# Four shared products of a Strassen-Winograd stage through one PSUM bank pair, sums moved from GpSimd to VectorE, and the first output steps prepared in another order

## The chip, the core and the metric

One core of a Trainium2 chip. The metric is the device time of one execution in microseconds, lower is better. Durations in the rows come from one profiled execution, counted from the start of its span.

## What is computed

```
scores = (q @ k.T) / 8, only where 0 <= query - key < 64, else -1e9      # 4 x 8 heads, 576 rows, 64 columns
x  = softmax(scores) @ v                                                # 2304 x 512
x2 = ((x @ w1) * (x @ w2)) @ w3 @ w_out                                 # 512 -> 1024 -> 512
h  = x2 @ w_in                                                          # 512 -> 2048
out = (h * sigmoid(h)) @ w_out2                                         # 2048 -> 512
```

Weights come in double precision and are turned to single on the chip.

## The kernel before, in words

Every matmul value is held as a high and a low part (float32r), and every product is made of three passes: high x high, high x low, low x high. The low part is the value minus its high part, a VectorE subtraction; the high part is a ScalarE cast.

The kernel has three stages. In the first, attention and the two gated layers run over six blocks of 384 tokens, TensorE drawing both. Then come h and its SiLU, then the output product. The change touches the last two, and the preparation of h's operands.

**The stage of h.** h = x2 @ w_in is done by a Strassen-Winograd scheme: operands are cut in quadrants, and seven products take the place of eight. There are 12 groups of seven products (`d`, called a duo in the code): `d // 4` is one of three super-blocks of 768 tokens, `d % 4` one of four parts of 512 columns of h. `product(d, k)` (L1005) is 12 matmuls of 384 columns: two halves, two contraction steps, three passes. Product `k` goes to the PSUM tile that `HOME` (L1003) names; there are four tiles, ha, hb, hc and hd, of two banks each, and together they fill PSUM. A product that is not `fresh` adds to what its tile holds. `read(d, k)` (L1031) takes the results out: ScalarE copies product 0 to `one` (L1038); product 2 adds to it in the bank, and SiLU of that sum is a11; VectorE makes `two` (product 1 plus `one`), adds product 3 to `one`, adds that to products 4 and 5, and product 6 to `two`; SiLU gives a12, a22 and `two`. `keep` (L1027) stores the four results to device memory (`gd`) through SP's queue.

The order is written out by hand. `POS` (L791) gives the product of each of the seven positions of a group; product 6 of a group runs at position 2 of the next group. `h_slot` (L1054) issues, for one position: the product, its read, low parts left from the last position (`run_later`), the jobs of that position (`run_jobs`), and at some positions stores. Every engine takes its instructions strictly in this order. Jobs are entered in a table by position number, 7 d + position, with `at` (L921): `w_part` prepares weights of h; `convert` (L876) turns w_out2 from double to single and makes its sums, one pair of rows every five positions from position 12, each a chain of loads on SP, scalings on ScalarE (L220, L225), bit operations on VectorE (L228, L884), an integer add on GpSimd (L887), sums and stores; `x_raw`, `x_sum` (L987) and `x_op` (L967) load the next super-block's x2, make its sums and split its seven operands; from position 56 on `o_load` and `o_part` (L955) load and split output weights.

**The output.** 36 steps, nine token groups of 256 by four parts of the contraction. `out_products(m)` (L1139) is 42 matmuls of 256 columns. Its operand is made from four stored quadrants: `f_load` (L1076) loads 512 KB, `f_sums` (L1090) makes four sums of 256 columns, `f_high` (L1101) casts and `f_low` (L1120) makes the low parts. In the steady loop these run three to six steps ahead. The first steps have an order of their own, written below the loop over `h_slot` (L1287 to L1313), since tile buffers are the places of h's operands and of a22, `two` and others.

## Time and profile before

| | us |
|---|---|
| median of 3 runs | 829.55 (829.38 to 831.58) |
| the profiled execution, its own time | 831.39 |
| its span on the core | 829.60 |
| first matmul of h, first of the output | 461.72, 637.04 |

The time of an execution holds the span and a little around it. "PE" is TensorE's matmuls, "PEld" its weight loads, DVE VectorE, ACT ScalarE, POOL GpSimd, SP the queue that issues most DMAs. A bracket at the end of a row says how long the engine stood before it and what ended that wait.

### The profile page before, as it was taken

How to read it: one execution, taken by the hardware profiler on the slowest of the kernel's cores; microseconds unless marked ns; L12 is line 12 of the kernel's file. 1: busy time of each engine (PE TensorE's matmuls, PEld its weight loads, DVE VectorE, ACT ScalarE, POOL GpSimd, SP SyncE). 2: the span in 40 equal slices, each digit the busy share in tenths (PEclk: the TensorE clock that was granted, in tenths of full speed). 3: DMA queues.
4: the chain of work that ended last, by engine and by line, in shares of the span. 5: the costliest groups of instructions: out<-in, count | busy, mean ns of one | idle time of the engine just before them, and what ended most of it. 6: DMA issues, size and time to landing. Idle time of an engine off the chain costs nothing.

```text
span 829.6 us, 15630 instructions
## 1 busy us (share of the span) xinstructions
PE 811.6 (98%) x5066; PEld 766.6 (92%) x5066; DVE 653.8 (79%) x1527; ACT 543.7 (66%) x1290; POOL 389.8 (47%) x468
## 2 busy tenths in 40 slices
PE   8899999999999999999999999999999899999998
PEld 3455799999999999999999999999999899999998
DVE  7878867788888888888557579977657999888882
ACT  6889878888899898899645456654555543444330
POOL 4768576667677677677644126444000112221100
PEclk9999999999999999999999999999999999999999
DMA  9998324534444545544132377896867555444421
GB/s 287 338 316 267 106 75 122 169 114 154 157 146 155 169 134 160 176 143 137 72 111 96 133 267 243 294 323 268 303 226 246 178 152 154 146 134 129 127 77 51
DMA packets 79792, 146.34 MB, mean 176 GB/s; under 512 B 7136, under 2 KB 46432, under 8 KB 79712
## 3 DMA queue, kind: packets, MB, share of 16 engines
q1 hardware_dynamic: 76112, 140.50, 51.7%
q10 hardware_dynamic: 3600, 4.85, 1.6%
q8 instruction: 40, 0.66, 0.3%
q14 instruction: 40, 0.33, 0.1%
HBM read 105.48 MB, written 39.85 MB: 175 GB/s over the span
## 4 chain that ended last, share of the span: by engine, by line
PE 66%; DVE 7%; ACT 7%; POOL 6%; issue 5%; DMA 1%; ACTq 0%; SPq 0%; DVEq 0%; POOLq 0%
PE ab L693 15%; PE oa L1160 11%; PE x L723 8%; PE ob L1160 8%; PE ha L1016 4%; PE hb L1016 4%; PE hd L1016 4%; PE hc L1016 2%; PE accw L614 2%; POOL klo L351 2%; PE t L428 2%; POOL vhl L369 1%; POOL p L117 1%; PE o L462 1%; POOL xr L474 1%
## 5 line engine op out<-in xcount | busy, mean ns | idle before, releaser
L693 PE MATMUL ab<-xa,hl 128*128 128x384 f32 x576 | 119.0, 341 | 0.0
L693 PE MATMUL ab<-xb,hl 128*128 128x384 f32 x570 | 115.2, 334 | 0.0
L693 PEld LDWEIGHTS ab<-xb,hl 128*128 128x128 f32 x570 | 100.3, 188 | 0.0
L693 PEld LDWEIGHTS ab<-xa,hl 128*128 128x128 f32 x576 | 99.1, 188 | 0.0
L1160 PE MATMUL oa<-wo_w,hi 128*128 128x256 f32 x408 | 77.9, 285 | 0.0
L351 POOL TENSOR_TENSOR klo<-qk,qkhi 64x192 fp32r<-64x192 f32 x110 | 67.3, 612 | 8.4 <-ACT qkhi L345 2.3
L723 PE MATMUL x<-p,wp 128*128 128x384 f32 x360 | 69.0, 339 | 0.0
L474 POOL TENSOR_TENSOR xr<-ot 128x128 f32<-128x128 f32 x55 | 32.7, 595 | 72.9 <-DVE ot L473 54.5
L800 POOL TENSOR_TENSOR fs<-f 128x256 f32<-128x256 f32 x11 | 9.8, 889 | 121.2 <-DMA f<-gd 99.7
L1160 PEld LDWEIGHTS oa<-wo_w,hi 128*128 128x128 f32 x408 | 63.6, 191 | 0.0
L723 PEld LDWEIGHTS x<-p,wp 128*128 128x128 f32 x360 | 61.8, 188 | 0.0
L1160 PE MATMUL oa<-wo_w,lo 128*128 128x256 f32 x204 | 58.3, 286 | 0.4 <-DVE lo L800 0.4
L406 ACT ACTIVATE sm<-sm,nm 128x192 f32<-128x192 f32 x110 | 49.3, 449 | 1.4
L1016 PE MATMUL ha<-xop,wi_w 128*128 128x384 f32 x252 | 47.8, 335 | 0.7 <-ACT gxb L1038 0.7
L1016 PE MATMUL hd<-xop,wi_w 128*128 128x384 f32 x252 | 47.7, 335 | 0.5 <-DVE gxb L800 0.5
L1016 PE MATMUL hb<-xop,wi_w 128*128 128x384 f32 x252 | 47.5, 334 | 0.0
L345 ACT CAST qkhi<-qk 128x768 fp32r<-128x768 f32 x55 | 46.0, 835 | 1.2
L392 DVE CUSTOM_DVE_ANT_0 sm<-s,consts 128x192 f32<-128x192 f32 x144 | 45.2, 352 | 1.3 <-PE s L385 0.8
L1016 PEld LDWEIGHTS ha<-xop,wi_w 128*128 128x128 f32 x252 | 44.0, 188 | 1.2 <-ACT gxb L1038 1.2
L1016 PEld LDWEIGHTS hd<-xop,wi_w 128*128 128x128 f32 x252 | 43.9, 188 | 0.8 <-DVE gxb L800 0.8
L1016 PEld LDWEIGHTS hb<-xop,wi_w 128*128 128x128 f32 x252 | 44.0, 188 | 0.0
L428 PE MATMUL t<-consts,sm 128*128 128x128 f32 x216 | 35.9, 275 | 7.4 <-DVE sm L418 5.3
(284 smaller groups left out, 2331.7 us busy)
## 6 DMA issues: line engine op xcount, KB each, us to landing
qk<-in_qkv SPq DMA_DIRECT2D x55, 384.0 KB, 3.0
words<-in_w3t SPq DMA_DIRECT2D x16, 512.0 KB, 6.4
words<-in_w SPq DMA_DIRECT2D x16, 512.0 KB, 6.6
xe<-in_w_in SPq DMA_DIRECT2D x16, 512.0 KB, 4.6
gq<-in_w_out SPq DMA_DIRECT2D x16, 512.0 KB, 4.5
gd<-gxa SPq DMA_DIRECT2D x18, 384.0 KB, 3.3
gd<-gst SPq DMA_DIRECT2D x18, 384.0 KB, 5.1
gq<-gd SPq DMA_DIRECT2D x13, 512.0 KB, 4.0
```

Source lines behind the costliest of these rows:

```text
L345: nc.scalar.copy(out=hi, in_=t)
L351: nc.gpsimd.tensor_tensor(out=k_lo[g % 2][hs, h * 192 : h * 192 + 192], in0=t[hs, n], in1=f32(hi[hs, n]), op=ALU.subtract)
L392: nc.vector.tensor_tensor_reduce(out=sm[g % 2][:, h, :], in0=s_ps[:, h, :], in1=consts[:, at + 64 - 64 * h : at + 256 - 64 * h], op0=ALU.a ...
L406: nc.scalar.activation(out=e[:, h, :], in_=x, func=AF.Exp, scale=-1.0, bias=nm[:, h : h + 1], accum_out=sums_of[g % 2][:, h, 0:1])
L428: nc.tensor.transpose(t_ps[:, i * 128 : i * 128 + 128], x[:, at : at + 128], id_sb)
L474: nc.gpsimd.tensor_tensor(out=xr[:, c, r : r + 128], in0=t[:, 0:128], in1=t[:, 128:256], op=ALU.add)
L614: nc.tensor.matmul(acc[i], lhsT=w3x[s % 7][:, i * 128 : (i + 1) * 128], rhs=wo[:, j], start=(j == 0), stop=(j == 7))
L693: nc.tensor.matmul(acc, lhsT=w[:, l, fs], rhs=x[k // 2][:, k % 2, r, :], start=(k == 0 and n == 0), stop=(k == 3 and n == 2),)
L723: nc.tensor.matmul(acc, lhsT=wp[f][:, l, o * 128 : (o + 1) * 128], rhs=p[f][:, r, :], start=(f == 0 and n == 0), stop=(f == 7 and n == 2),)
L800: eng.tensor_tensor(out=out, in0=a, in1=b, op=op)
L1016: nc.tensor.matmul(bank[name][:, q, 0:NB], lhsT=w[:, l, first + kt], rhs=x[:, kt, r, :], start=(fresh and kt == 0 and n == 0), stop=(kt == ...
L1160: nc.tensor.matmul(dst, lhsT=lhs[l], rhs=rhs[r], start=(first and e == 0 and q == 0 and n == 0), stop=(e == DUOS - 1 and q == 1 and n == 2 ...
```

## The change

- Products 0, 1, 3 and 4 of a group all go to one tile, ha for even groups and hb for odd ones, and add up there. Between them ScalarE copies the running sum out: product 0 to `one`, 0+1 to `two`, 0+1+3 to a22; SiLU of the whole is a12. Product 2 is alone in hc and gets `one` by a VectorE add; products 5 and 6 share hd as before.
- The order is now 0, 4 of the group before, 1, 6 of the group before, 2, 5, 3. Product 5 is read behind product 0 of the next group. In the first group the positions that would hold products of a group before are empty or closed up. a22 and a12 are stored at position 3 instead of 0, `two` at 5 instead of 4, a11 at 6 instead of 4.
- The x sums and the first sum of each output tile go to VectorE; so do the two sums that GpSimd made for each of h's weight tiles 4 to 7 (L863, L866). The integer adds and sums of the conversions stay on GpSimd.
- The operands of the next super-block are split in the order 0, 1, 2, 5, 3, 4, 6, most a position later.
- The first output tile is loaded at position 14 of the last four groups instead of 22, summed at 17 instead of 24 and split at 24 and 25 instead of 25 and 26; the second is summed and cast before the end of h. Buffers of the tiles change places, and some begin 16 columns further in theirs (`shifted`). After the loop the order is: step 0, products 4 and 6 of the last group, step 1, with splits and weights between them (before: step 0, product 6, step 1). The first output step uses ha and hc.

```diff
--- before.py
+++ after.py
@@ -98,7 +98,7 @@
     SLOTS = {"p": 4096, "q": 2304, "xa": 1536, "xb": 1536, "xr": 1536, "st": 1024, "x2": 4096, "cv_r": 512, "cv_b": 512}
-    SLOTS.update({"xe": 2304, **{f"x{i}": 1536 for i in range(7)}})
+    SLOTS.update({"xe": 2304, **{f"x{i}": 1568 if i < 6 else 1536 for i in range(7)}})
@@ -788,7 +788,7 @@
         OPS = 7
-        POS = (0, 1, 6, 2, 4, 3, 5)
+        POS = (0, 4, 1, 6, 2, 5, 3)
         HALF = slice(0, NB), slice(NB, 2 * NB)
@@ -860,10 +860,10 @@
                 add(nc.vector, a22, a21, a22)
-                sub(nc.gpsimd, a21, a11, a21)
+                sub(nc.vector if n > 3 else nc.gpsimd, a21, a11, a21)
             elif part == 3:
                 sub(nc.vector, a11, a22, a11)
-                sub(nc.gpsimd, a12, a12, a11)
+                sub(nc.vector if n > 3 else nc.gpsimd, a12, a12, a11)
             elif part == 4:
@@ -931,8 +931,8 @@
                 t = [xe[:, 0:1024], xe[:, 1024:1536], xe[:, 1536:1792]]
-            elif n == 6:
-                x = slot("or6", "x0", [1536], pool=end)
+            elif n == 7:
+                x = slot("or7", "xb", [1536])
                 t = [x[:, 0:1024], x[:, 1024:1536], st[3][:, 768:1024]]
@@ -990,23 +990,26 @@
             if i == 0:
-                sub(nc.gpsimd, tmp["t1"], b12, b11)
+                sub(nc.vector, tmp["t1"], b12, b11)
             elif i == 1:
...
             elif i == 2:
-                sub(nc.gpsimd, b12, b22, b12)
+                sub(nc.vector, b12, b22, b12)
             else:
...
         WHERE = ((0, 0, 0), (2, 0, 1), (0, 2, 2), (1, 0, 3), (3, 0, 4), (1, 2, 5), (2, 2, 6))
-        HOME = ("ha", "hb", "ha", "hb", "hc", "hd", "hd")
+        HOME = ("hx", "hx", "hc", "hx", "hx", "hd", "hd")
+        def home(d, k):
+            return ("ha", "hb")[d % 2] if HOME[k] == "hx" else HOME[k]
...
             j, e = divmod(d, DUOS)
-            x, name = xop[j, i], HOME[k]
-            fresh = k in (0, 1, 4, 5)
+            x, name = xop[j, i], home(d, k)
+            fresh = k in (0, 2, 5)
             if fresh:
@@ -1033,42 +1036,43 @@
-            one, two = g["one"], g["two", d % 2]
-            if k == 0:
-                nc.scalar.copy(out=one, in_=h_bank("ha"))
-            elif k == 1:
-                add(nc.vector, two, h_bank("hb"), one)
+            src, two = h_bank(home(d, k)), g["two", d % 2]
+            if k in (0, 1, 3):
+                nc.scalar.copy(out={0: g["one"], 1: two, 3: g["a22"]}[k], in_=src)
             elif k == 2:
-                silu(g["a11"], h_bank("ha"))
-            elif k == 3:
-                add(nc.vector, one, h_bank("hb"), one)
-                add(nc.vector, h_bank("hc"), h_bank("hc"), one)
-                silu(g["a12"], h_bank("hc"))
+                add(nc.vector, g["a11"], src, g["one"])
+                silu(g["a11"], g["a11"])
+            elif k == 4:
+                silu(g["a12"], src)
             elif k == 5:
-                add(nc.vector, g["a22"], h_bank("hd"), one)
+                add(nc.vector, g["a22"], src, g["a22"])
                 silu(g["a22"], g["a22"])
             elif k == 6:
-                add(nc.vector, two, h_bank("hd"), two)
+                add(nc.vector, two, src, two)
                 silu(two, two)
...
             k = POS[pos]
-            if k == 6:
-                if d:
-                    product(d - 1, 6)
-                    read(d - 1, 6)
-            else:
+            if d == 0:
+                k = (0, 2, 1, None, 5, 3, None)[pos]
+            if k in (4, 6):
+                product(d - 1, k)
+                read(d - 1, k)
+            elif k is not None:
                 product(d, k)
-                read(d, k)
+                if k != 5:
+                    read(d, k)
+            if pos == 0 and d:
+                read(d - 1, 5)
             run_later()
             run_jobs(7 * d + pos)
-            if pos == 0 and d:
+            if pos == 3 and d:
+                keep(d - 1, 2, g["a22"])
                 keep(d - 1, 1, g["a12"])
-                keep(d - 1, 2, g["a22"])
-            elif pos == 4:
+            elif pos == 5 and d:
+                keep(d - 1, 3, g["two", 1 - d % 2])
+            elif pos == 6:
                 keep(d, 0, g["a11"])
-                if d:
-                    keep(d - 1, 3, g["two", 1 - d % 2])
@@ -1076,9 +1080,9 @@
                 return
-            if m and (m == 1 or m % 3 == 0):
+            if m == 0 or m % 3 == 2:
                 t = xe[:, 0:1024], xe[:, 1024:2048]
-            elif m % 3 == 1:
+            elif m > 1 and m % 3 == 1:
                 t = slot(f"f{m}", "w21", [1024]), slot(f"fs{m}", "w22", [1024])
@@ -1087,16 +1091,22 @@
-        def f_sums(m, eng=None):
+        def f_sums(m):
...
                 f, t = [x.rearrange("p (a n) -> p a n", a=4) for x in raw["f", m]]
-                add(eng or nc.gpsimd, t[:, 0], f[:, 3], f[:, 2])
+                add(nc.vector, t[:, 0], f[:, 3], f[:, 2])
                 sub(nc.vector, t[:, 1], f[:, 3], f[:, 0])
...
                 sub(nc.vector, t[:, 3], f[:, 1], t[:, 2])
+        def shifted(name, tag):
+            t = slot(name, tag, [SLOTS[tag]], F32R, end)
+            t = t[:, 16:1552] if SLOTS[tag] > 1536 else t
+            return t.rearrange("p (a n) -> p a n", a=6)
@@ -1107,9 +1117,9 @@
                         tmp["a11"] = slot("a11", "xr", [3, 512], F32R)
-                    lo = slot(f"lo{m}", ("x2", "x4", "x0")[n], [6, 256], F32R, end)
+                    lo = shifted(f"lo{m}", ("x1", "x5", "x4")[n])
                     a = tmp["a11"][:, n]
-                hi = slot(f"hi{m}", ("x1", "x3", "x5", "x6")[n], [6, 256], F32R, end)
+                hi = shifted(f"hi{m}", ("x0", "x2", "x3", "x6")[n])
                 a = [a[:, 0:256], a[:, 256:512]]
@@ -1140,7 +1150,7 @@
             if e == 0:
-                for x, y in (("a", "ha"), ("b", "hb"), ("c", "hc")) if tg % 2 == 0 else (("a", "hc"), ("b", "hd")):
+                for x, y in (("a", "ha"), ("b", "hc"), ("c", "hb")) if tg % 2 == 0 else (("a", "hb"), ("b", "hd")):
                     if x != "c" or last:
@@ -1250,22 +1260,21 @@
             at(s + 5, x_sum, 2)
-            for k, f, x in ((8, x_op, 0), (9, x_sum, 1), (9, x_op, 1), (11, x_op, 2), (12, x_sum, 3), (12, x_op, 3)):
+            for k, f, x in ((8, x_op, 0), (9, x_sum, 1), (10, x_op, 1), (12, x_op, 2), (13, x_sum, 3), (13, x_op, 5)):
                 at(s + k, *((f, j, x) if f is x_op else (f, x)))
-            for k, x in ((13, 4), (14, 5), (17, 6)):
+            for k, x in ((14, 3), (16, 4), (18, 6)):
                 at(s + k, x_op, j, x)
...
         FIRST_OUT = 7 * DUOS * (SUPER - 1)
-        for n, first in ((0, 2), (1, 10), (2, 12), (3, 16), (4, 18), (5, 23), (6, 26)):
-            for part in range(4 if n < 6 else 2):
+        for n, first in ((0, 2), (1, 10), (2, 12), (3, 17), (4, 19), (5, 25)):
+            for part in range(4 if n < 5 else 3):
                 at(FIRST_OUT + first + part, o_part, n, part)
-        for n, first in ((0, 0), (1, 6), (2, 6), (3, 13), (4, 16), (5, 20), (6, 22)):
+        for n, first in ((0, 0), (1, 6), (2, 6), (3, 13), (4, 16), (5, 21)):
             at(FIRST_OUT + first, o_load, n)
-        for k, f, m in ((22, f_load, 0), (22, f_load, 1), (25, f_high, 0), (26, f_low, 0)):
+        for k, f, m in ((14, f_load, 0), (17, f_sums, 0), (23, f_load, 1), (24, f_high, 0), (25, f_low, 0)):
             jobs.setdefault(FIRST_OUT + k, []).insert(0, lambda f=f, m=m: f(m))
-        jobs.setdefault(FIRST_OUT + 24, []).insert(0, lambda: f_sums(0, nc.vector))
-        at(FIRST_OUT + 26, f_load, 2)
-        at(FIRST_OUT + 27, o_load, 7)
+        for k, f, m in ((26, f_load, 2), (26, f_sums, 1), (27, f_high, 1)):
+            at(FIRST_OUT + k, f, m)
@@ -1287,29 +1296,34 @@
                 h_slot(d, pos)
+        last = NDUO - 1
         run_later()
-        f_sums(1, nc.vector)
-        f_high(1)
         f_low(1)
+        read(last, 5)
+        f_load(3)
+        f_load(4)
         out_products(0)
-        keep(NDUO - 1, 1, g["a12"])
-        keep(NDUO - 1, 2, g["a22"])
-        o_part(6, 2)
-        o_part(6, 3)
-        f_sums(2, nc.vector)
+        o_part(5, 3)
+        o_load(6)
+        keep(last, 2, g["a22"])
+        f_sums(2)
+        product(last, 4)
+        product(last, 6)
+        read(last, 4)
+        f_sums(3)
+        for part in range(4):
+            o_part(6, part)
+        keep(last, 1, g["a12"])
+        o_load(7)
         f_high(2)
+        read(last, 6)
+        keep(last, 3, g["two", last % 2])
         f_low(2)
-        f_load(3)
-        product(NDUO - 1, 6)
-        read(NDUO - 1, 6)
-        keep(NDUO - 1, 3, g["two", 1 - NDUO % 2])
+        f_load(5)
         for part in range(4):
             o_part(7, part)
-        f_sums(3, nc.vector)
         f_high(3)
         f_low(3)
-        f_load(4)
-        f_load(5)
         f_load(6)
```

## Rows read from the trace of the kernel before

**Rows 1.** The page: busy time of each engine, share of the span, instructions.

```profile
PE 811.6 (98%) x5066; PEld 766.6 (92%) x5066; DVE 653.8 (79%) x1527; ACT 543.7 (66%) x1290; POOL 389.8 (47%) x468
```

**Rows 2.** TensorE in order of time, stage of h: start, length, what.

```profile
461.72 2.24 PE L1016 MATMUL ha<-xop,wi_w 128*128 128x384 f32 x12
463.80 2.24 PE L1016 MATMUL hb<-xop,wi_w 128*128 128x384 f32 x12
...
507.37 0.97 PE L1016 MATMUL hb<-xop,wi_p 128*128 128x384 f32 x4 [0.41 <-DVE wi_p L800]
508.84 2.37 PE L1016 MATMUL hd<-xop,wi_w 128*128 128x384 f32 x12 [0.50 <-DVE gxb L800]
...
521.45 2.24 PE L1016 MATMUL hb<-xop,wi_w 128*128 128x384 f32 x12
...
526.49 2.37 PE L1016 MATMUL ha<-xop,wi_w 128*128 128x384 f32 x12 [0.72 <-ACT gxb L1038]
```

**Rows 3.** By stretch: us, busy PE PEld DVE ACT POOL, clock, DMA, GB/s.

```profile
497.00:530.00 33.00, 31.38 (x178) 30.39 (x177) 32.20 (x41) 20.19 (x30) 18.76 (x16) 1.00 0.75 255
659.50:663.00 3.50, 3.50 (x19) 3.50 (x18) 3.43 (x7) 2.56 (x5) 1.60 (x2) 0.51 0.37 132
...
700.00:750.00 50.00, 50.00 (x419) 50.00 (x418) 43.88 (x77) 19.27 (x34) 11.41 (x11) 1.00 0.46 145
```

**Rows 4.** TensorE in order of time, end of h and first output steps.

```profile
637.04 0.40 PE L1160 MATMUL ob<-o0b,hi 128*128 128x256 f32 x2
638.26 0.39 PE L1160 MATMUL ob<-o0b,lo 128*128 128x256 f32 x1 [0.82 <-DVE lo L800]
...
645.38 0.40 PE L1160 MATMUL ob<-wo_w,hi 128*128 128x256 f32 x2
...
650.40 0.40 PE L1160 MATMUL ob<-wo_w,hi 128*128 128x256 f32 x2
...
657.51 0.39 PE L1160 MATMUL ob<-wo_w,lo 128*128 128x256 f32 x1 [1.67 <-DVE lo L800]
...
664.60 0.41 PE L1160 MATMUL ob<-o0b,hi 128*128 128x256 f32 x2
```

**Rows 5.** Groups of instructions by form: count, busy us, mean ns, idle before.

```profile
L1038 ACT COPY gxb<-ha 128x768 f32<-128x768 f32 x12 | 9.5, 790 | 1.7 <-PE ha L1016 1.6
L971 ACT CAST xop<-xe 128x768 fp32r<-128x768 f32 x8 | 6.6, 826 | 0.0
L220 ACT ACTIVATE cv_b<-gq 128x512 f32<-128x512 f32 x16 | 10.7, 670 | 7.7 <-DMA gq<-in_w_out 5.9 <-issue 1.8
L800 DVE TENSOR_TENSOR gxb<-hd,gxb 128x768 f32<-128x768 f32 x11 | 10.4, 950 | 0.0
L800 DVE TENSOR_TENSOR wo_w<-gq,wo_w 128x512 fp32r<-128x512 f32 x6 | 3.9, 686 | 0.0
L800 POOL TENSOR_TENSOR xe<-xra 128x768 f32<-128x768 f32 x2 | 4.6, 2300 | 0.0
...
L884 DVE SCALAR_TENSOR_TENSOR cv_b<-gq,cv_b 128x512 int32<-128x512 int32 x6 | 4.1, 683 | 0.0
```

**Rows 6.** VectorE in order of time, near 501 and near 647.

```profile
501.41 2.07 DVE L800 TENSOR_TENSOR cv_t<-cv_b,cv_t 128x256 f32<-128x256 f32 x1
...
646.98 1.55 DVE L800 TENSOR_TENSOR gq<-gq 128x256 f32<-128x256 f32 x4
648.45 1.82 DVE L800 TENSOR_TENSOR lo<-gq,hi 128x768 fp32r<-128x768 f32 x2
```

**Rows 7.** ScalarE in order of time: two copies of product 0, and a SiLU.

```profile
464.00 0.80 ACT L1038 COPY gxb<-ha 128x768 f32<-128x768 f32 x1 [1.60 <-PE ha L1016]
...
523.04 0.85 ACT L1025 ACTIVATE gxb<-gxb 128x768 f32<-128x768 f32 x1 [1.74 <-DVE gxb L800]
...
525.66 0.78 ACT L1038 COPY gxb<-ha 128x768 f32<-128x768 f32 x1
```

**Rows 8.** Stores of a22 (tile gxb) in the stage of h, issue to landing.

```profile
DMA to landing us min/median/max: 2.5/5.2/8.9
```

## The prediction

> **What bounds the kernel now.** I read the shares first: TensorE is busy for 98% of the span, VectorE 79%, ScalarE 66% [rows 1]. Whatever the other engines save, the time can only fall by what TensorE spends standing or at a low clock, so the next view is TensorE's own order of time. In the stage of h a product of 12 matmuls is followed by the next after 2.08 us (461.72 to 463.80). From 461.72 to the first output matmul at 637.04 there are 83 products, 172.6 us, and it takes 175.3: **2.7 us are lost**, at 507 to 509 (a weight part late from VectorE, then bank hd held by a VectorE add) and at 526.49 (bank ha held by a ScalarE copy) [rows 2]. The table by stretches shows why: around them VectorE is busy 32.2 of 33.0 us [rows 3].
>
> An output step is 42 matmuls and takes 5.02 us (645.38 to 650.40). From 637.04 to 664.60 stand four steps and one product, 4 x 5.02 + 2.08 = 22.2 us, and it takes 27.6: **5.4 us are lost**. TensorE's rows say why: 638.26 and 657.51 both wait for VectorE's low parts (0.82 and 1.67 us) [rows 4], and after the second the granted clock is 0.51 (the 1.2 GHz level) from 659.5 to 663.0, where the other stretches show 1.00; what had gone before is the standing at 655 to 659. Behind that there is nothing to win: 50.00 of 50 us busy [rows 3]. So 8.0 us are in reach.
>
> **The change part by part.**
>
> *Reads of h.* A group of seven products (14.56 us) had one ScalarE copy, four SiLUs and five VectorE adds; it gets three copies, four SiLUs, three adds. VectorE loses 2 x 0.95 = 1.9 us a group, ScalarE gains 2 x 0.79 = 1.6 [rows 5]. For the 33 us from 497 that is 4.3 off VectorE's 32.2 and 3.6 on ScalarE's 20.2 [rows 3]: VectorE has room again, ScalarE stays at 72%.
>
> *Sums for h.* Two x sums of 768 columns per later super-block go to VectorE, about 0.95 each (nearest row, an add of this size). The first took GpSimd 2.30 us [rows 5], and beside it a VectorE sum of 256 columns took 2.07 us at 501.41, where four such take 1.55 when GpSimd rests [rows 6]. I count 1.9 added and as much given back: 0. The eight weight sums, 0.39 each, make 3.1 more, but they lie at positions 3 to 16, before that stretch, where VectorE still waits for products: 0, and up to 3.1 of delay for the weights without that room. So the weight part that TensorE waits for at 507.37 comes earlier, and the 2.7 us go; bounds 0 (VectorE's backlog is the conversions') and 2.7. The first super-block's sums lie in the last attention block, covered by four accumulators in turn; without that cover they cost 1.9.
>
> *Handovers.* In one bank, product 1 must follow the copy of product 0, and product 4 the copy of product 3, each with one other product (2.08 us) between; product 5 follows the add of product 6 with one between too. Before, at least two lay between. A copy starts 0.20 us after the next product's start (464.00 against 463.80) and takes 0.80 [rows 2, 7], so TensorE waits only if it starts more than 1.05 late. ScalarE's queue from product 3's end: copy until 1.0, then the jobs of position 6, at most an x operand (0.83) and two conversion scalings (0.67 each, nearest row) [rows 5], until 3.2; the copy of product 0 is wanted at 2.28 and may start at 3.3. It fits by a hair. In the old order it started at 525.66, 4.2 us after its product's last issue at 521.45, since a SiLU that waits for a VectorE add (523.04) stood ahead of it [rows 2, 7]; the new order issues that SiLU behind it. Lowest price 0; highest is the first rival's; I take 0.5, one handover late as at 526.49.
>
> The Trainium skill ("Perfetto Trace Analysis", Matmuls) says that independent matmul groups should rotate through different PSUM banks, so that the evacuation of one overlaps the next group's matmuls. By that rule the copies would stand on TensorE's path; the old trace, with longer gaps between, has one such wait (526.49) and can't show more.
>
> *The store of a22.* The copy of product 3 overwrites a22, whose store must have landed. The store moves from position 0 to position 3, on SP behind the conversions' loads and stores, and the overwrite moves up from the fifth product's add to the third's copy. In group 4 SP first issues a load that needs a VectorE sign step queued behind the add of product 6: 8.3 + 0.2 + 0.95, a low part 0.95 and the step 0.7 [rows 5] make 11.1 us after the group's start. The store goes out at 11.4 and lands 2.5, 5.2 or 8.9 us later [rows 8]: 13.9, 16.6, 20.3. TensorE needs the copy begun by 14.56 + 1.25 = 15.8. So it costs 0, 0.8 or 4.5; I take 0.8. In group 3 SP is free about 1.7 us earlier, so there only the longest costs.
>
> *Start of the output.* Tile 0 is loaded eight positions earlier and split two products before the end, so the stand at 638 goes. Then come step 0, products 4 and 6, steps 1 to 3: step 3 starts 19.2 us after the last product of the loop instead of 17.2. VectorE must by then do three splits (1.82 + 0.39), two sets of sums (1.55), two adds (0.95) and two and a half sets of weights (about 2.4 each: three of 0.69 and one of 0.39) [rows 5, 6]: 17.6 us. It was four splits, three sets of sums, three adds and as many weights: 22.3 in 17.2, hence the loss. What is late next, counted from that last product's end: the last weights are loaded into the space of a22, after its store. SiLU at 5.8, store landed near 10.5, load landed 4 to 5 later near 15, then casts, split casts and a low part, about 4.9: 19.9, so step 3 stands 0.7 us. Bounds 0 and 4.1 (the loss at 657 with its slow clock). SP's other moved loads go out when their buffers come free, ahead of use by two slots or more: 0.
>
> *Sums of the output on VectorE.* A step needs 1.55 + 2.2 and about 0.65 for a quarter of the final sums, 4.4 of 5.02 us. It has 43.88 of 50 now, beside GpSimd [rows 3], so removing GpSimd pays for the added sum: 0. Without that, 0.39 more a step still fits (95%).
>
> Sum: -8.0 + 0.5 + 0.8 + 0.7 = -6.0. The profiled execution took 831.39 with a span of 829.60; the median of the runs shown is 829.55, 1.8 lower. I take the difference off the median: **823.5**.
>
> **The rivals.**
>
> 1. *The bank chain stalls (slower).* ScalarE's copies come late at half of the 23 handovers, by 1 us beyond the slack: 12 x 1.0. 829.55 - 8.0 + 1.5 + 12 = 835. Above 0.28 us a handover ((8.0 - 1.5) / 23) it is slower than before. For it: the copy's history at 525.66, ScalarE's jobs in strict order, loads that its jobs wait for. Against: the SiLU now stands behind. The Trainium skill's rule on rotating banks speaks for this one. Chance 0.08.
> 2. *Stalls only move.* The store of a22 or the start of the output costs its upper end: -8.0 + 0.5 + 4.5 + 0.7 gives 827.2, the other 826.9. Chance 0.16. Both: 830.6, chance 0.04.
> 3. *The backlog stays.* VectorE in 497 to 530 is full of the conversions whatever the reads cost, so the change doesn't do that part: the 2.7 us stay, 826.2. Chance 0.14; against it, 4.3 us of 32 go.
>
> **How the numbers follow.** The forecast has 0.58, alone 821.5 to 825.5. A measurement of this kernel tells 0.3% (2.5 us) from no change: faster is below 827.1, slower above 832.0. Forecast, the third rival and half of the second's single case (0.58 + 0.14 + 0.08) are faster: 0.80. The other half and half of the double case are the same: 0.08 + 0.02 = 0.10. The first rival and the other half of the double case are slower: 0.10. The range starts where all 8.0 us are saved, 821.5, and goes to 828.3, past the second rival's single case; what it leaves out is the first rival and the double case.
>
> **What would show it.** TensorE's timeline from 461 on: 84 products and no wait over 0.2 us for VectorE, apart from one or two of some 0.5 to 1 us on a ScalarE copy into gxb (a22) near groups 3 and 4, with the store of gxb as what ended ScalarE's wait. VectorE near 28 of 33 us in the stretch of 497. No wait before the first output step; one under 1 us at step 3, for a low part; no stretch with the clock at half. In steady output steps VectorE's share as before, GpSimd at 0, and the same 5.02 us a step, though the operand tiles lie 16 columns further (no row prices that; I take 0). I'd be wrong if waits on a ScalarE copy recur in most groups, or if the granted clock still falls near 660.

## The result, and the profile after

The changed kernel takes **821.18 us** (median of 6 runs, 820.65 to 823.86) against 830.52 for the kernel before on the same chip (829.38 to 831.58): ratio 0.9895, 95% interval 0.9878 to 0.9913, about 9.3 us faster. I had forecast 6.0 us of gain, and 823.5 us, in a range from 821.5 to 828.3. So the side was right, and the gain is larger than the forecast: it is more than the 8.0 us that I had called in reach, and the median lies 0.3 us under the range's lower end. The profiled execution took 821.25 us, with a span of 819.3; before it was 831.39 and 829.60.

First the share of busy time, which answers to [rows 1]:

```profile
PE 804.2 (98%) x5066; PEld 760.5 (93%) x5066; DVE 633.0 (77%) x1549; ACT 562.8 (69%) x1314; POOL 340.2 (42%) x422
```

TensorE executes the same 5066 matmuls in 7.4 us less busy time. Some 1.7 of it, by my estimate, is the stretch at half the clock that is gone (3.5 us at 0.51); the rest is the first sign that something other than waits has changed, since work that only stops waiting doesn't get shorter.

TensorE in order of time in the stage of h (answers to [rows 2]; start, length, what, and in brackets the wait before it). These two waits are all that it has there:

```profile
487.86 2.25 PE L1019 MATMUL hb<-xop,wi_w 128*128 128x384 f32 x12
490.36 2.38 PE L1019 MATMUL ha<-xop,wi_w 128*128 128x384 f32 x12 [0.25 <-ACT gxb L1041]
```

```profile
530.30 2.25 PE L1019 MATMUL hb<-xop,wi_w 128*128 128x384 f32 x12
532.76 2.35 PE L1019 MATMUL ha<-xop,wi_w 128*128 128x384 f32 x12 [0.21 <-ACT gxb L1041]
```

The bracket counts only the time that TensorE stood; the loss is read from the starts. 490.36 - 487.86 = 2.50 us, and the product behind takes 2.22, where one takes 2.08: 0.56 lost. At 532.76 it is 0.49 in the same way. Both waits are for a ScalarE copy into gxb (`one` and a22), the handover in the shared tile.

By stretch (answers to [rows 3]; us, busy time of PE, PEld, DVE, ACT, POOL with instructions, granted clock, DMA share, GB/s):

```profile
497.00:530.00 33.00, 33.00 (x191) 33.00 (x190) 27.45 (x39) 25.54 (x39) 14.19 (x13) 1.00 0.85 289
700.00:750.00 50.00, 50.00 (x435) 50.00 (x435) 44.94 (x93) 20.41 (x34) 0.00 (x0) 1.00 0.49 148
659.50:663.00 3.50, 3.50 (x33) 3.50 (x32) 3.47 (x8) 1.97 (x4) 0.00 (x0) 1.00 0.50 150
```

VectorE fell from 32.20 to 27.45 of 33 us, TensorE stands nowhere in that stretch, and the clock stays at its upper level (1.00, 2.4 GHz) around 660. The row to stop at is the second: in 50 us that TensorE fills in either kernel, it now starts 435 matmuls, not 419.

The start of the output (answers to [rows 4]):

```profile
633.46 0.40 PE L1170 MATMUL ob<-o0b,hi 128*128 128x256 f32 x2
...
647.76 0.50 PE L1170 MATMUL ob<-wo_w,hi 128*128 128x256 f32 x2 [0.33 <-ACT hi L1127]
...
649.68 0.38 PE L1170 MATMUL ob<-wo_w,lo 128*128 128x256 f32 x1 [1.42 <-DVE lo L800]
...
659.73 0.40 PE L1170 MATMUL ob<-o0b,hi 128*128 128x256 f32 x2
664.54 0.40 PE L1170 MATMUL ob<-wo_w,hi 128*128 128x256 f32 x2
669.36 0.39 PE L1170 MATMUL ob<-wo_w,hi 128*128 128x256 f32 x2
...
674.16 0.40 PE L1170 MATMUL ob<-wo_w,hi 128*128 128x256 f32 x2
...
679.20 0.40 PE L1170 MATMUL ob<-o0b,hi 128*128 128x256 f32 x2
```

No wait at the first step, a stand at step 2 (647.76 and 649.68), and then steps of 4.81, 4.82, 4.80 and 5.04 us, where all had taken 5.04. The pattern repeats to the end: a step whose m mod 4 is 3 keeps 5.04. Those are the steps whose operand tiles lie in places that were not widened and so are not shifted by 16 columns.

Between the profiled executions 10.3 us are gone. Before h 1.1 (461.72 to 460.61). Of the stage before, only the first super-block's sums are part of the change, and h starts anywhere from 460.1 to 461.1 us in the experiments' traces (e2, in the old order, at 461.1), so I don't count this as a gain of the change. From h's first matmul to step 4 3.8 (202.88 to 199.12). From step 4 to the end of the span 5.4 (165.00 to 159.57), **over half of the gain, in a stretch where I had written that there is nothing to win**.

### The profile page after: what moved, and what is told of

The parts are those of the page before. It is cut to its first block, busy times and chain, and to the rows that moved or that the text cites. A ratio compares the mean times of both kernels' runs of the same rounds, so it can differ in the third digit from the quotient of the medians.

```text
span 819.3 us, 15577 instructions
## 1 busy us (share of the span) xinstructions
PE 804.2 (98%) x5066; PEld 760.5 (93%) x5066; DVE 633.0 (77%) x1549; ACT 562.8 (69%) x1314; POOL 340.2 (42%) x422
## 4 chain that ended last, share of the span: by engine, by line
PE 72%; POOL 6%; ACT 6%; issue 4%; DVE 2%; DMA 2%; SPq 0%; ACTq 0%; POOLq 0%; DVEq 0%
PE ab L693 16%; PE oa L1170 11%; PE x L723 9%; PE ob L1170 8%; PE ha L1019 6%; PE hd L1019 6%; PE hb L1019 5%; PE hc L1019 3%; PE accw L614 2%; POOL klo L351 2%; PE t L428 2%; POOL vhl L369 1%; POOL p L117 1%; POOL xr L474 1%; PE o L462 1%
## 5 line engine op out<-in xcount | busy, mean ns | idle before, releaser
L1170 PE MATMUL oa<-wo_w,hi 128*128 128x256 f32 x408 | 74.3, 277 | 0.0
L1170 PEld LDWEIGHTS oa<-wo_w,hi 128*128 128x128 f32 x408 | 61.8, 188 | 0.0
L1019 PE MATMUL ha<-xop,wi_w 128*128 128x384 f32 x288 | 54.4, 337 | 0.5 <-ACT gxb L1041 0.5
L1019 PEld LDWEIGHTS ha<-xop,wi_w 128*128 128x128 f32 x288 | 50.5, 188 | 1.1 <-ACT gxb L1041 1.1
L887 POOL TENSOR_TENSOR cv_b<-cv_b,cv_r 128x512 int32<-128x512 int32 x16 | 22.3, 1394 | 62.7 <-DVE cv_b L884 50.9
L1170 PE MATMUL ob<-wo_w,hi 128*128 128x256 f32 x216 | 40.8, 278 | 0.3 <-ACT hi L1127 0.3
L723 PE MATMUL x<-q,wp 128*128 128x384 f32 x210 | 40.3, 334 | 0.0
```

What stands on the lines that cost most here:

```text
L723: nc.tensor.matmul(acc, lhsT=wp[f][:, l, o * 128 : (o + 1) * 128], rhs=p[f][:, r, :], start=(f == 0 and n == 0), stop=(f == 7 and n == 2),)
L887: nc.gpsimd.tensor_tensor(out=c.b, in0=c.b, in1=c.r, op=ALU.add)
L1019: nc.tensor.matmul(bank[name][:, q, 0:NB], lhsT=w[:, l, first + kt], rhs=x[:, kt, r, :], start=(fresh and kt == 0 and n == 0), stop=(kt == ...
L1170: nc.tensor.matmul(dst, lhsT=lhs[l], rhs=rhs[r], start=(first and e == 0 and q == 0 and n == 0), stop=(e == DUOS - 1 and q == 1 and n == 2 ...
```

## The experiments

**1 and 2: the 16 columns.** Only this part was taken out of the changed kernel, and then only this part put into the kernel before.

```diff
# e1: the changed kernel
-    SLOTS.update({"xe": 2304, **{f"x{i}": 1568 if i < 6 else 1536 for i in range(7)}})
+    SLOTS.update({"xe": 2304, **{f"x{i}": 1536 for i in range(7)}})
# e2: the kernel before
+            t = slot(name, tag, [SLOTS[tag]], F32R, end)
+            t = t[:, 16:1552] if SLOTS[tag] > 1536 else t
```

> The changed kernel with the places of the x operands back at 1536 columns, so that the operand tiles of the output begin at the start of their places again; all else is the change. Theory (the 16 columns make the matmuls of the output start closer together): steps with tile number 0, 1 or 2 modulo 4 go from 4.81 back to 5.04 us, 27 of 36 steps, so 6 us more: about 827 us; products 1, 3 and 5 of h, which take 2.11 us in the changed kernel, go back to 2.08, 1.3 us less, so 826. Rival (it is GpSimd's silence that makes the output's matmuls faster): steps stay at 4.81 and the time at 820 to 821.

> The kernel before with nothing but the wider places and the 16 columns for the output's operand tiles. Theory (the offset): 27 steps at 4.81 us, h's products 1, 3 and 5 at 2.11, waits at 507, 526, 638 and 657 as they were: 830.5 - 6.1 + 1.3 = about 825.7. Rival (GpSimd): no change, 830 to 831, with steps of 5.04.

Without the shift the changed kernel takes 825.99 us (ratio to before 0.9953, 0.9938 to 0.9969); the shift alone brings the kernel before to 824.94 (0.9937, 0.9920 to 0.9953), from 830.04 beside it. In e1 every steady step takes 5.04 us again, in e2 three of four take 4.80. The stretch from 700 to 750 us, e1 and then e2:

```profile
700.00:750.00 50.00, 50.00 (x419) 50.00 (x418) 42.53 (x87) 19.96 (x34) 0.00 (x0) 1.00 0.44 137
700.00:750.00 50.00, 50.00 (x435) 50.00 (x434) 48.09 (x84) 21.42 (x35) 10.29 (x11) 1.00 0.49 155
```

GpSimd is silent in e1, with 419 matmuls, and works in e2, with 435: so its silence is not what shortens the steps. The shift is worth 4.8 to 5.2 us, and it needs nothing else of the change. Turned round, the rest of the change without the shift is worth 4.1 us (830.04 to 825.99).

(Lines of the experiments' traces can lie one to three off those of the changed kernel.)

**3 to 6: what about the place counts?** The output's shifted tiles are a matmul's stationary operand; the weights move past them. By their sizes (1568 columns are 24.5 times 256 bytes) the widened places begin alternately 0 and 128 bytes off where they began before, modulo 256 bytes. Distances here are counted from those old places, since no trace shows an address. h's products 1, 3 and 5 read the odd ones, and take 2.11 to 2.12 us. Four edits vary one distance each (e1 has all at 0):

```diff
# e5: h's x operands of products 1, 3, 5 at column 32 of their places
+            c = 32 if i in (1, 3, 5) else 0
+            t = xop[j, i] = t[:, c : c + 1536].rearrange("p (a b n) -> p a b n", a=2, b=2)
# e6: h's x operands 0 to 5 at column 16
+            c = 16 if i < 6 else 0
# e7: the output's tiles at columns of their own
+            c = {"x0": 16, "x1": 32, "x2": 0, "x5": 16, "x3": 0, "x4": 32}.get(tag, 0)
# e9: places as in e1, and all of the main pool (the weights among it) 64 bytes further
+    pad = main.tile([128, 16], F32, name="pad", tag="pad")
```

> The x operands of products 1, 3 and 5 start at column 32 of their places, so that every x operand starts at a multiple of 256 bytes again; the offset of the output's operand tiles stays. Theory: the place of a matmul's operand sets the 2.11 us of products 1, 3 and 5 in the changed kernel (2.08 for 0, 2, 4, 6). Then all take 2.08, 36 x 0.035 = 1.3 us go, and the time is about 819.9 us. Rival: the 0.035 us are a cost of VectorE's added sums (reads of SBUF beside TensorE), not of the place: the three products stay at 2.11 and the time at 821.2.

> The x operands of products 0 to 5 start at column 16 of their places, as the output's tiles do; nothing else is changed. Theory A: 64 bytes between the starts of the two operands of a matmul is what counts, whichever of them moves. Then the 384-column matmuls of h, 173 ns each, get shorter by the output's share or the output's nanoseconds (7 ns of 120: 7 to 10 ns), 72 products x 12 matmuls x 7 to 10 ns = 6 to 9 us, and the time is 812 to 815 us. Theory B: in the output the shifted tiles are the stationary operands, and only their place counts. Then h stays between 2.08 and 2.11 us a product, and the time is 820 to 823 us.

> Output steps with m mod 4 = 0 have the high tile alone 64 bytes off (its low tile at a multiple of 256 bytes), those with 1 the low tile alone, those with 2 have both tiles at an odd multiple of 128 bytes, those with 3 neither, as before. Theory: each matmul is shortened by the place of its own stationary tile. Two of three passes read the high tile, so steps 0 take 5.04 - 2/3 x 0.23 = 4.89 us, steps 1 4.96, and steps 2 and 3 5.04 if 64 bytes are what counts; over 9 steps of each kind that is 0.7 + 1.4 + 2.1 = 4.2 us more than the changed kernel, 825.4. Rival: 128 bytes do as well as 64: steps 2 take 4.81 and the time is 823.3. Second rival: the distance of the two stationary tiles from each other is what counts: steps 0 and 1 both take 4.81 or so, and the time is 823.3 with steps 2 at 5.04.

> All places of x are 1536 columns again and no tile of the output is shifted (as in the experiment without the offset, 826.0 us); instead a tile of 16 columns stands first in the main pool, so that everything in that pool (the weights of h and of the output, the blocks and weights of the stage before h) lies 64 bytes further, and nothing in the pool on the other side (the x operands, the output's tiles of tokens) does. Theory A, the distance between the two operands counts: h gets shorter by 32 of 416 cycles' half, 6.7 ns of 173 in 1008 matmuls = 6.7 us; the output's steps take 4.81 and those with m mod 4 = 3, whose low tile lies in the main pool, 4.96 (5.04 without any offset): 27 x 0.23 + 9 x 0.08 = 6.9 us; the stage before h is unchanged, since both its operands move: 812.4 us. Theory B, the start of the stationary operand itself counts: h gains the same 6.7 us, the stage before h too (some 1716 matmuls of 173 ns, 11.4 us), the output nothing but in the steps with m mod 4 = 3: 807 to 808 us. Theory C, 384-column matmuls don't gain at all: 819 us (the output alone, by distance) or 826 us (nothing).

e5 takes 820.38 us (0.9883, 0.9868 to 0.9897). That is 0.8 under the changed kernel by the medians, with intervals that overlap; the trace is plainer. Products 2, 1, 5, 3 of the first group, e5:

```profile
462.42 2.24 PE L1021 MATMUL hc<-xop,wi_w 128*128 128x384 f32 x12
464.50 2.24 PE L1021 MATMUL ha<-xop,wi_w 128*128 128x384 f32 x12
466.58 2.24 PE L1021 MATMUL hd<-xop,wi_w 128*128 128x384 f32 x12
468.66 2.24 PE L1021 MATMUL ha<-xop,wi_w 128*128 128x384 f32 x12
```

and in the changed kernel:

```profile
462.69 2.24 PE L1019 MATMUL hc<-xop,wi_w 128*128 128x384 f32 x12
464.77 2.28 PE L1019 MATMUL ha<-xop,wi_w 128*128 128x384 f32 x12
466.89 2.27 PE L1019 MATMUL hd<-xop,wi_w 128*128 128x384 f32 x12
469.00 2.28 PE L1019 MATMUL ha<-xop,wi_w 128*128 128x384 f32 x12
```

In e5 the starts are 2.08 apart; in the changed kernel product 1 takes 466.89 - 464.77 = 2.12. So widening the places costs h 36 products of 0.035 us, 1.3 us, and the place does it.

e6 takes 821.50 us (0.9896, 0.9881 to 0.9910): theory B's number. Products 0, 2 and 4 stay at 2.08, and 1, 3, 5 take 2.10. The 384-column matmuls don't get shorter with 64 bytes between the operands.

e7 takes 825.71 us (0.9950, 0.9935 to 0.9965), as the theory's sum said, but not by its parts. Steps with m mod 4 = 0, 1, 2, 3, and the next 0:

```profile
662.22 0.40 PE L1171 MATMUL ob<-o0b,hi 128*128 128x256 f32 x2
...
667.18 0.40 PE L1171 MATMUL ob<-wo_w,hi 128*128 128x256 f32 x2
...
672.14 0.39 PE L1171 MATMUL ob<-wo_w,hi 128*128 128x256 f32 x2
...
677.13 0.40 PE L1171 MATMUL ob<-wo_w,hi 128*128 128x256 f32 x2
...
682.17 0.40 PE L1171 MATMUL ob<-o0b,hi 128*128 128x256 f32 x2
```

High tile alone 64 bytes off: 4.96 (I had said 4.89). Low tile alone: 4.96. Both 128 bytes off: 4.99. None: 5.04. In the starts of single matmuls, a step with the low tile alone has 113 ns from every third matmul, its low pass, to the next and 119 to 121 from the others; one with the high tile alone has 117 to 118 from all three. So the high tile gives half of what "each matmul by its own tile" asks for, and that part of the theory falls.

e9 separates "where the stationary tile begins" from "how far the two operands are apart", since here the stationary tiles stay and the weights move. It takes 820.81 us (0.9890, 0.9873 to 0.9907), near the 819 of theory C with distance:

```profile
660.53 0.39 PE L1172 MATMUL ob<-o0b,hi 128*128 128x256 f32 x2
...
665.33 0.39 PE L1172 MATMUL ob<-wo_w,hi 128*128 128x256 f32 x2
...
670.13 0.39 PE L1172 MATMUL ob<-wo_w,hi 128*128 128x256 f32 x2
674.93 0.39 PE L1172 MATMUL ob<-wo_w,hi 128*128 128x256 f32 x2
...
679.89 0.39 PE L1172 MATMUL ob<-o0b,hi 128*128 128x256 f32 x2
```

Three steps of 4.80, and 4.96 for the fourth, whose low tile moved with the weights. So in steady steps the distance counts, not the place. h takes 2.10 a product against 2.08 in e1, 1.3 us in all, so it loses a little; the stage before h, where both operands moved, stays at 173 to 174 ns a matmul of 384 columns. The distance isn't all, though: e9's steps 0 and 1 have 118 ns a matmul, with the same tiles as the later steps that have 113.

**7 and 8: the sums that left GpSimd.** The sums of x, of h's weights 4 to 7 and of the output's tiles went back to GpSimd; two of the five places:

```diff
-                sub(nc.vector, tmp["t1"], b12, b11)
+                sub(nc.gpsimd, tmp["t1"], b12, b11)
...
-                add(nc.vector, t[:, 0], f[:, 3], f[:, 2])
+                add(nc.gpsimd if m > 3 else nc.vector, t[:, 0], f[:, 3], f[:, 2])
```

> The changed kernel with the x sums, the weight sums and, from the fifth tile on, the first sum of each output tile back on GpSimd. If these sums were what filled VectorE near 507: VectorE above 30 of 33 us busy from 497 and some of the 2.7 us of waits in h back, 1 to 3 us slower than the change. If it was the two adds a group that the reads of h lose: no wait of h on VectorE, within 0.5 us of the change. Steps of the output stay at 4.81 either way unless GpSimd is what shortens them.

> The changed kernel with the first sums of x, of the output's weights and of the output's tiles on GpSimd again, for its trace: 823.3 us by the runs before. Theory A: the 2 us are waits at the handovers in h and at the start of the output (GpSimd's sums end later, and VectorE's queue behind them), so the first output step starts later than 633.5 us or its first four steps take longer than 26.3 us, and the steady steps stay at 4.81 us. Theory B: GpSimd's work beside VectorE lengthens the steady steps (32 of them, 0.06 us each), with h and the start as in the changed kernel.

The first took 823.28 us (0.9915, 0.9899 to 0.9932); the second, one run for its trace, 822.51. The steady steps are unchanged at 4.81, so theory B is out. The stretch of 497, of the second:

```profile
497.00:530.00 33.00, 33.00 (x190) 32.75 (x189) 28.92 (x36) 25.01 (x37) 19.53 (x16) 1.00 0.85 279
```

VectorE is busy 28.92 of 33 us, not above 30, and TensorE waits for it nowhere in h: the relief near 507 doesn't need the moved sums. It came with the reads and their new order, which no run takes apart. VectorE is also no less busy without these sums (27.45 with them, in a window that doesn't hold quite the same work).

From h's first matmul to the output's it takes 174.4 us against 172.85, and over half of that is one handover in h. TensorE and ScalarE there:

```profile
491.43 2.38 PE L1019 MATMUL ha<-xop,wi_w 128*128 128x384 f32 x12 [1.10 <-ACT gxb L1041]
```

```profile
490.03 0.67 ACT L220 ACTIVATE cv_b<-gq 128x512 f32<-128x512 f32 x1 [0.78 <-DMA gq<-in_w_out]
490.60 0.78 ACT L1041 COPY gxb<-ha 128x768 f32<-128x768 f32 x1
```

The copy of product 0 stands behind a conversion scaling that waits for its load. In the changed kernel the same scaling starts at 488.94 without a wait, and the load is issued at nearly the same time in both (482.81 and 482.59). So what is late is a transfer, and no row ties it to GpSimd's sums; the intervals of the two kernels overlap as well. Whether the sums cost anything where they were stays open, between 0 and 2 us.

**9 to 11: the stand in step 2.** ScalarE and then VectorE at the start of the output of the changed kernel:

```profile
640.60 0.81 ACT L1028 ACTIVATE gst<-hb 128x768 f32<-128x768 f32 x1 [1.12 <-PE hb L1019]
645.00 1.97 ACT L962 CAST wo_w<-gst 128x512 fp32r<-128x512 f32 x4 [3.59 <-DMA gst<-t]
646.88 1.56 ACT L1127 CAST hi<-xe 128x768 fp32r<-128x768 f32 x2
```

```profile
645.66 2.23 DVE L800 TENSOR_TENSOR wo_w<-gst,wo_w 128x512 fp32r<-128x512 f32 x4 [3.19 <-ACT wo_w L962]
647.81 0.95 DVE L800 TENSOR_TENSOR gxa<-hd,gxa 128x768 f32<-128x768 f32 x1
648.67 1.82 DVE L800 TENSOR_TENSOR lo<-xe,hi 128x768 fp32r<-128x768 f32 x2
```

The sums of tile 2 (xe) were done at 641.0, but its cast stands behind the casts of weights 6, whose load landed at 645.0. VectorE holds it up in the same way: the low parts of tile 2, which TensorE's longer wait (1.42 us) is for, stand behind those of weights 6 and behind the last add of h. Three orders were tried (`read(6)` is the last add and SiLU of h, with its store):

```diff
# e4
         product(last, 6)
         read(last, 4)
+        f_high(2)
+        f_low(2)
         f_sums(3)
+        read(last, 6)
+        keep(last, 1, g["a12"])
+        keep(last, 3, g["two", last % 2])
         for part in range(4):
             o_part(6, part)
-        keep(last, 1, g["a12"])
         o_load(7)
-        f_high(2)
-        read(last, 6)
-        keep(last, 3, g["two", last % 2])
-        f_low(2)
# e8, in that place
         f_sums(3)
         keep(last, 1, g["a12"])
         f_high(2)
         read(last, 6)
         keep(last, 3, g["two", last % 2])
         f_low(2)
         o_load(7)
         for part in range(4):
             o_part(6, part)
         f_load(5)
         f_high(3)
         f_low(3)
         for part in range(4):
             o_part(7, part)
# e10: e8, with the load of weights 7 in other buffers
-                x = slot("or7", "xb", [1536])
-                t = [x[:, 0:1024], x[:, 1024:1536], st[3][:, 768:1024]]
+                t = [st[1], xb[:, 0, 0:512], st[3][:, 768:1024]]
```

> The changed kernel with the third tile cast and split before the weights of pair 6 are cast, and the read of product 6 behind that split. Theory (step 2 stands because ScalarE waits for the load of weights 6 in front of the cast of tile 2): the 0.3 and 1.4 us at step 2 go, about 2 us with the restart, and 819 us results, unless step 3 then waits for weights 7, whose load waits for the store of a22: then up to 1 us stands there. Rival (VectorE is short of time in that stretch): the wait moves to step 3 whole and the time stays at 821.

> At the start of the output the split of tile 2 and the last combine of h stand ahead of the split of weights 6, the split of tile 3 ahead of that of weights 7; the load of weights 7 stays ahead of nothing it was not ahead of, and behind the store of the last combine, which is issued some 645 us in, before the load can start anyway (647). Theory: the stand of 2.2 us in step 2 is ScalarE's wait for the load of weights 6 in front of the cast of tile 2. Without it step 2 runs through and step 3 stands 0 to 1 us for weights 7: 819.0 to 820.0 us. Rival: the weights' loads are what is late and the wait only moves to step 3, whole: 821.2 us, with about 2 us of stand there.

> As the experiment on the output's start, with the load of weights 7 put into buffers that are free by 636 us (of the combines 'one' and 'two' of the even pairs) instead of the one whose store it waited for until 647 us. Theory: the stand of 1.5 us in step 3 was this load (landed at 652.3). With it landed by 648, step 3 runs through: 818.5 to 819.0 us. Rival: DMA is 0.94 busy from 640 to 654, so the load arrives no earlier than before, or the load of weights 6 gets later beside it and step 2 stands instead: 820.4 us or more.

e4 takes 826.64 us (0.9957, 0.9942 to 0.9972), 5.5 slower than the changed kernel, which neither theory had. Step 2 runs through, and step 3 stands (TensorE, then SP's queue):

```profile
656.26 0.50 PE L1170 MATMUL ob<-wo_w,hi 128*128 128x256 f32 x2 [3.21 <-ACT hi L1127]
```

```profile
642.26 0.38 SPq L1032 DMA_DIRECT2D gd<-gst  x1
648.39 0.32 SPq L1032 DMA_DIRECT2D gd<-gxa  x1
648.80 1.78 SPq L941 DMA_DIRECT2D or<-t  x2
```

I had moved a store ahead of the load of weights 7. It waits for the last SiLU (gxa, 647.52), whose add waits behind VectorE's split of tile 2 and sums of tile 3, so the load goes out at 648.80 and not at 646.99 (1.0 us later, counted from the output's first matmul), ScalarE's casts wait for it until 653.51, and the cast of tile 3 waits behind them. The granted clock falls to 0.69 from 656 to 660 besides.

e8 has the last SiLU ahead of the split, and the store is out by 644.73. It takes 820.37 us (0.9882, 0.9865 to 0.9898). Steps 1 and 2 run through (4.83, 4.80); step 3 takes 6.51, a loss of 1.5 us for weights 7. Their load goes out when it did in the changed kernel (646.98) and lands 1.9 us later (652.28 against 650.40). From the output's first matmul to step 4: 25.1 us, before the edit 26.3. By the medians the time lies between the theory's number and the rival's, and the interval overlaps that of the changed kernel, so the gain is read from the trace alone.

e10 takes 820.36 us (0.9875, 0.9857 to 0.9894): by its median the rival's number. In its trace step 3 takes 5.47, and from the first matmul to step 4 pass 24.1 us; but h took 0.9 longer in that execution than in the changed kernel's. And the edit did less than I meant, as SP's queue shows:

```profile
645.78 0.32 SPq L1031 DMA_DIRECT2D gd<-gxa  x1
646.15 0.42 SPq L940 DMA_DIRECT2D gst<-t  x1
```

The load no longer waits for a buffer, but it still stands behind the store of the last SiLU, and goes out 0.8 us earlier, not 6. In both traces the casts of weights 7 start at 652.28 and step 4 at 658.81, since h ended 1.05 us later in e10's. So e10 alone doesn't refute its rival, a load that arrives no earlier; e12, whose output begins at 633.54 as e8's does at 633.68, has these casts at 650.61.

**12: the repairs together** (e5's and e10's edits).

> The two repairs together: x operands of products 1, 3 and 5 at the weights' place (h's 2.11 us back to 2.08), and the start of the output with the splits of tiles 2 and 3 ahead and the load of weights 7 in free buffers. If they add up: 1.0 us (the first alone, by its median) and 0.8 us (the second alone) under the changed kernel's 821.2: 819.4 us; by the traces alone, 1.3 and 2.2 us, 817.7. Rival: what is saved before the output comes back as a stand in its steps 2 and 3, whose loads are issued by a fixed time: 820.4 us, with more than the 0.4 us of stand in step 3 that the second repair left.

**818.76 us**, ratio 0.9856 (0.9840 to 0.9873): better than both kernels, its interval lying wholly under that of the changed kernel. The expectation had 819.4 us by the medians and 817.7 by the traces, if the two add up, and 820.4 for the rival: the time lies between the two sums, and the rival is out. Output steps 1 to 3 take 4.83, 4.80 and 5.04 us, with no stand. What TensorE waits for from h's start to step 4 is two handovers (engine, line, waited for: us in total, times, longest):

```profile
PE ha L1020 <- ACT gxb L1042: 0.4, 1, 0.4
PE hb L1020 <- ACT gxb L1042: 0.2, 1, 0.2
```

By the starts, 1.9 us are still lost at handovers in h (172.49 us for 82 products of 2.08).

## Why the prediction was right, and where it was wrong

**The 8.0 us in reach: right, but new waits took back more than I had said.** The waits at 507 to 509 and 526 are gone, so is the one at 638, and so is the slow clock behind 657. That clock wasn't a fixed price of the stand, though: in e2 the same stand (2.01 and 0.43 us, at 657.93 and 659.34) is followed by a granted clock of 1.00 up to 670. Without the 16 columns (e1) the parts that I had priced come to 4.1 us by the medians and 4.4 by the traces from h's first matmul on, where I had said 6.0. So part of the forecast's nearness is luck: handovers and the start of the output took more than I gave them, and a gain that I had put at nothing more than made up for it. VectorE in the stretch of 497 came to 27.45 of 33 us, where I had said near 28; ScalarE came to 77%, where I had said 72%.

**Handovers and the store of a22: right in kind, rather small in size.** I took 0.5 + 0.8 = 1.3 us; the profiled execution lost 0.56 + 0.49 = 1.05. One is a copy of product 0 behind ScalarE's jobs, three casts of weights and a conversion scaling from 487.60 on. The other is a copy of product 3 that waited 0.28 us for the store of a22, behind a scaling that had waited 0.72 for its load. But this is the least of ten traces: in the nine others with this order of h and these sums (e1, e4 to e10, e12) the stage lost 1.4 to 2.4 us, at the same two places and at a third near 563 us (e5: 172.92 us for 82 products of 2.08). The Trainium skill ("Perfetto Trace Analysis", Matmuls) says to rotate PSUM banks between independent matmul groups. Here four products that add up, and so aren't independent, shared a tile with one other product between; the trace shows a wait of the kind that the rule is meant to avoid at two of 23 handovers, for about 1 us in all. So the first rival fell, though the two waits are of its kind.

**The start of the output: the term that was mis-sized.** I wrote that step 3 stands 0.7 us, bounds 0 and 4.1. Step 3 did not stand; step 2 did, and the stretch lost 2.6 us: 26.3 from 633.46 to 659.73, for two products (4.16) and steps of 3 x 4.81 + 5.04. The step that failed is "What is late next". I counted VectorE's work and the chain of the last weights through the space of a22, and left out that the casts of weights 6, which wait for a load, stand ahead of tile 2's cast on ScalarE, and their low parts ahead of tile 2's on VectorE. The chain that I did count was real: it is the stand of step 3 in e8, once the other one is gone.

**Steady steps: wrong, and the largest error.** I wrote "the same 5.02 us a step, though the operand tiles lie 16 columns further (no row prices that; I take 0)". It measured -0.23 us in three steps of four, and against it +0.035 in three products of seven in h. e1 and e2 put the two together at 4.8 to 5.2 us. I had kept no bounds for this edit, neither a gain nor a loss, though I had just said that no row shows it. With it the sum comes out, by the traces from h's first matmul on: -8.0, + 1.0 (handovers), + 2.6 (start of the output), + 1.3 (products of h), - 0.7 (steps 0 to 2), - 5.4 (steps from 4 on) is -9.2, and measured were 3.8 + 5.4 = 9.2.

**Sums on VectorE: 0 predicted.** Not refuted: the steady steps have the same length either way, and TensorE waits for VectorE in h neither with the sums there nor without. Over half of what the trace of e11 loses in h against the changed kernel is a wait for a transfer.

## What to carry to other kernels

When an edit moves a tile by a few columns, don't price it at nothing: take the spacing of the same matmuls before and after, and try a pad of 16 columns ahead of one operand, which costs one line and here gave 5 us (and look at the other matmuls that share the buffers: in h the same columns cost 1.3 us). Where a wait is taken out by a new order, follow every queue that the moved lines pass through, ScalarE's and SP's as well: in e4 and in e10 a store in front of a load set the result. A stand that moves by one step, as from step 2 to step 3 here, has a second cause behind it: e8 took out the first, and neither e8 nor e10 can be told from the changed kernel by its interval; e12, which joins e10 with the repair of h, can.

## What the runs showed of the hardware

In steady output steps the spacing of float32r matmuls with 256 columns went with the distance between the start of the stationary tile and that of the moving one, counted from the places before: 120 ns at 0 (e1), 113 ns with both stationary tiles 64 bytes to either side (the changed kernel) or the weights moved by 64 bytes (e9), 119 on average at 128 bytes (e7). At 2.4 GHz 120 and 113 ns are 288 and 272 cycles for 256 columns. The distance isn't all: at the same distances e9's steps 0 and 1 have 118 ns and its later ones 113, and step 2 of the changed kernel has 119 behind its stand, where step 6 has 113. In e6, with a like stand, step 2 has 113. What makes the difference stays open.

Matmuls with 384 columns take 173 ns (416 cycles) at distance 0 (e1) and 64 bytes to one side (products 0, 2 and 4 of e6), 175 at 64 bytes to the other (1, 3 and 5 of e6, all of h in e9) and 176 at 128 (the changed kernel): none of these distances shortened them. Why the wider ones don't gain, and why the high tile alone shortens all three passes by a little, no run here shows. In the changed kernel the fourth kind of output step and the products with the sums S4, which stay at 120 ns, were not shifted; e9 moved the high tile of the fourth kind alone, for 4.96 us, and what both tiles or S4 would give was not tried.
